# Streaming V in 8 MB tiles, wq in one load, and a tail with narrow last rows, in a one-core decode kernel

## The chip, the cores and the metric

The kernel runs on one core of one Trainium2 chip. The metric is the device time of one execution in microseconds (us). Before the change it was 405.86 us, the median of three runs (405.73 to 405.91). A profiled execution also has a span, from its first to its last instruction, which is some 1.8 us shorter than the time (404.1 against 405.84 us). "Clock" below is the granted clock of TensorE (PE), 1.0 for full and 0.5 for half. The other engines are DVE (VectorE), ACT (ScalarE) and POOL (GpSimd); PEld is the weight load of PE.

## The reference, cut to what matters

One token passes through an attention block (32 query heads, 4 KV heads, 65,536 cached keys of 128 values) and, beside it, a two-layer MLP. Both are added to the input.

```python
xn = layernorm(x)                                   # x: [1, 1, 1024] bf16
q = xn @ wq                                         # wq: [1024, 4096], 8.4 MB
p = softmax(q k^T * 128**-0.5)                      # k_cache: 67 MB
attn = (p @ v) @ wo                                 # v_cache: 67 MB, wo 8.4 MB
h = gelu(layernorm(xn) @ w1) ; x1 = xn + shift(h) @ w2   # shift: zero for one token
mlp = x1 + gelu(layernorm(x1) @ w3) @ w4            # w3, w4: 7.3 MB each
out = x + attn + mlp
```

Every byte of K, V and the weights is read once: 169.87 MB by the profile's count of its load queue. There is very little arithmetic per byte.

## The kernel before

All loads are issued on one queue in a fixed stream. K, V, wq, w3 and w4 share five tiles of 4 MB (32 KB per partition). The smaller matrices use one 2 MB tile. A load is issued as soon as its buffer is free.

```python
UKEYS = 16384
BIG_BUFS = 5
W4_PIECES = ((8, 8), (8, 2, 1, 1))
...
stream = [("wq", 0), ("wq", 1), ("w3", 0), ("w3", 1), ("w1", 0), ("K", 0), ("K", 1), ("V", 0)]
for u in range(2, NU):
    stream += [("K", u), ("V", u - 1)]
...
stream += [("wo", HKV - 1), ("V", NU - 1), ("w4", 0), ("w4", 1)]
...
src = cache[0, g, b * UKEYS:(b + 1) * UKEYS, :].rearrange("(p ct) d -> p (ct d)", p=P)
nc.sync.dma_start(out=t[:], in_=src)
```

The output is accumulated in psB, one tile of PSUM (the memory into which the matmuls write), whose rows 0 and 32 hold the two halves of the 1024 outputs. Each row of w2, wo and w4 adds two matmuls of 512 columns. w4 comes last, in pieces of 8, 8, 8, 2, 1 and 1 rows of 256 KB each, so that little work is left after the last byte.

```python
def row_acc(j, lhsT, rhs):
    nc.tensor.matmul(psB[32 * j:32 * j + 1, :], lhsT=lhsT, rhs=rhs, start=False, stop=False,
                     tile_position=(0, 32 * j), skip_group_check=True)
...
compute_w4(0, W4_PIECES[0][0])
compute_w4(1)
out_t = ppool.tile([64, 512], BF16, name="out_t", tag="p_sb")
nc.scalar.copy(out=out_t[:], in_=psB[0:64, :])
nc.scalar.dma_start(out=out[0, 0, :].rearrange("(j n) -> j n", j=2), in_=...)
```

## Time and profile before

| what | before |
|---|---|
| time, median | 405.86 us |
| span of the profiled execution | 404.1 us |
| data packets per DMA engine | 384 |
| load queue, first packet to last byte | 1.74 to 399.68: 397.94 us |
| of which packets fill, mean of 16 engines | 396.34 us |
| last byte to end of span | 4.37 us |

The last four rows are counted from the trace's records of single DMA packets. The window is the time from the first packet to the last byte. The packets leave 1.6 us of it empty, so faster compute could shorten it by no more than that. It is set by bytes and by the cost per packet.

Lines of the page of the kernel before: busy time of each engine, then, in 40 equal slices, the granted clock of PE in tenths and the busy share of the DMA engines in tenths, then the load queue.

```profile
span 404.1 us, 3287 instructions
PE 236.2 (58%) x1392; PEld 94.1 (23%) x1392; DVE 211.8 (52%) x241; ACT 34.3 (8%) x61; POOL 6.4 (2%) x19
...
PEclk9998558688897979797978979596959895879769
DMA  8999999999999999999999999999999999999993
...
q1 hardware_dynamic: 6912, 169.87, 98.1%
```

The DMA row is at 9 from the second slice to the second to last. No compute engine is busy for more than 58%.

The chain of waits of the kernel before (start, length, what), with its first piece, one of the long ones, and its end:

```profile
0.74 12.40 DMA x_bf<-in_A_x_dram
...
140.77 46.33 DMA big<-in_A_k_cache_dram
...
355.04 42.55 DMA big<-in_B_w_dram
397.63 2.93 PE psB L179 x24
400.58 0.58 ACT out_t L526
```

The chain ends in the last weight load and then in 24 matmuls. The timeline of the same stretch (start, length, engine, line, operation, output and inputs, count, and the idle time before):

```profile
394.19 1.89 PE L179 MATMUL psB<-big,cols_h 128*1 128x512 bf16 x16
...
397.63 2.91 PE L179 MATMUL psB<-big,cols_h 128*1 128x512 bf16 x24 [1.55 <-DMA big<-in_B_w_dram]
...
400.58 0.58 ACT L526 CAST out_t<-psB 64x512 bf16<-64x512 f32 x1 [25.40 <-PE psB L179]
401.19 0.61 ACTq L527 DMA_DIRECT2D out_dram<-out_t  x1
```

The last 24 matmuls took 2.9 us, about 0.12 us each, and kept pace with the last pieces. The busy time by stretch shows the clock they had (the column after POOL is the granted clock):

```profile
core 0: us, PE busy (x) PEld busy (x) DVE busy (x) ACT busy (x) POOL busy (x), PEclk, DMA share, GB/s
396.00:398.00 2.00, 0.45 (x6) 0.17 (x5) 0.00 (x0) 0.00 (x0) 0.00 (x0) 1.00 0.71 266
398.00:400.00 2.00, 2.00 (x22) 0.79 (x17) 0.00 (x0) 0.00 (x0) 0.00 (x0) 1.00 0.18 68
```

It was full.

### The profile page before, as it was taken

What the parts mean: (1) busy time and instruction counts of PE and PEld (TensorE: products, weight loads), DVE (VectorE), ACT (ScalarE), POOL (GpSimd) and SP (SyncE); (2) the same over time, 40 slices, a digit from 0 to 9 for tenths busy, and PEclk for the clock granted to TensorE, in tenths of its full rate; (3) what the DMA queues carried; (4) which work ended last, traced back from release to release, by engine and by line L of the source; (5) the groups of instructions that cost most, each with busy time, mean ns of one, the idle gap of its engine ahead of it and who ended that gap; (6) DMA issues with size and microseconds to landing.
All of it is one profiled execution on the core that took longest, in us unless ns stands there. A gap on an engine that the chain in (4) does not pass through costs nothing.

```text
span 404.1 us, 3287 instructions
## 1 busy us (share of the span) xinstructions
PE 236.2 (58%) x1392; PEld 94.1 (23%) x1392; DVE 211.8 (52%) x241; ACT 34.3 (8%) x61; POOL 6.4 (2%) x19
## 2 busy tenths in 40 slices
PE   0382727839483859292929394565658561948094
PEld 0131202313131323031313231122213220313041
DVE  0310046957658584566585473738393934665310
ACT  1000210110101011001010101010101010010100
POOL 4000100000000000000000000000000000000000
PEclk9998558688897979797978979596959895879769
DMA  8999999999999999999999999999999999999993
GB/s 357 422 415 431 449 416 439 440 418 429 448 417 425 454 409 430 444 431 417 448 428 418 436 420 438 428 444 423 428 436 428 422 436 435 431 426 430 420 427 144
DMA packets 7237, 170.11 MB, mean 421 GB/s; under 512 B 1070, under 2 KB 1074, under 8 KB 1462
## 3 DMA queue, kind: packets, MB, share of 16 engines
q1 hardware_dynamic: 6912, 169.87, 98.1%
q8 instruction: 11, 0.18, 0.2%
q0 software_dynamic: 160, 0.02, 0.0%
q10 hardware_dynamic: 150, 0.01, 0.0%
q14 instruction: 4, 0.03, 0.0%
HBM read 169.88 MB, written 0.01 MB: 420 GB/s over the span
## 4 chain that ended last, share of the span: by engine, by line
DMA 49%; PE 30%; DVE 10%; another core or an unknown queue 6%; ACT 2%; issue 2%; SPq 0%; DVEq 0%; ACTq 0%
DMA big<-in_A_k_cache_dram 35%; PE sc L383 21%; DMA big<-in_B_w_dram 11%; DVE big L372 5%; PE oacc L457 4%; DMA x_bf<-in_A_x_dram 3%; DVE s_sb L390 2%; PE psq L250 1%; ACT p_sb L421 1%; PE psB L179 1%; PE psB L239 1%; DVE pT L424 1%; PE pm_mx L400 1%; DVE og L439 0%
## 5 line engine op out<-in xcount | busy, mean ns | idle before, releaser
L383 PE MATMUL sc<-big,qdiag 128*128 128x512 bf16 x512 | 150.0, 461 | 104.9 <-DVE big L372 104.9
L372 DVE STREAM_TRANSPOSE big<-big 128x2048 f32<-128x2048 f32 x64 | 142.4, 2279 | 49.4 <-DMA big<-in_A_k_cache_dram 49.4
L383 PEld LDWEIGHTS <-qdiag 128*128 128x128 bf16 x512 | 56.8, 111 | 193.2 <-issue 100.3
L457 PE MATMUL oacc<-big,pT 128*32 128x512 bf16 x512 | 37.7, 396 | 9.7 <-DMA big<-in_A_v_cache_dram 9.7
L390 DVE TENSOR_SCALAR_CACHE_REDUCE s_sb<-sc 128x1024 f32<-128x1024 f32 x16 | 19.6, 1225 | 45.0 <-PE sc L383 45.0
L424 DVE STREAM_TRANSPOSE pT<-p_sb 128x1024 bf16<-128x1024 bf16 x16 | 19.8, 1240 | 16.8 <-ACT p_sb L421 16.8
L463 ACT COPY ob<-oacc 128x512 f32<-128x512 f32 x12 | 7.0, 586 | 214.6 <-PE oacc L457 214.6
L421 ACT ACTIVATE p_sb<-s_sb,nball 128x1024 bf16<-128x1024 f32 x16 | 18.4, 1150 | 76.5 <-DVE nball L419 76.5
L457 PEld LDWEIGHTS <-pT 128*32 128x32 bf16 x512 | 14.0, 99 | 28.7 <-issue 17.1
L400 PE MATMUL pm_mx<-ident_f,mx 128*1 128x128 f32 x16 | 4.3, 270 | 16.7 <-DVE s_sb L390 16.7
L419 DVE COPY nball<-pm_mx 128x1 f32<-128x1 f32 x16 | 2.5, 153 | 17.5 <-PE pm_mx L413 17.5
L250 PE MATMUL psh<-big,ln_rep_b 128*32 128x512 bf16 x56 | 5.5, 505 | 8.8 <-DMA big<-in_B_w_dram 8.8
L466 DVE SCALAR_TENSOR_TENSOR og<-oacc,wb,og 128x512 f32<-128x512 f32 x4 | 3.0, 751 | 12.5 <-PE oacc L457 12.5
L179 PE MATMUL psB<-big,cols_h 128*1 128x512 bf16 x56 | 7.7, 420 | 1.6 <-DMA big<-in_B_w_dram 1.6
L189 PE MATMUL pm_ln<-ln_rowsum_a,ones_f 128*128 128x1 f32 x2 | 0.6, 348 | 13.7 <-DVE sel L213 13.7
L179 PE MATMUL psB<-w,oT 128*1 128x512 bf16 x64 | 7.6, 379 | 0.0
L473 PE MATMUL pm_e<-og,selbig 128*128 128x128 f32 x32 | 5.6, 326 | 3.2 <-DVE nball L419 2.3
L402 DVE TENSOR_REDUCE negm<-pm_mx 1x8 f32<-1x128 f32 x16 | 4.4, 275 | 5.4 <-PE pm_mx L400 5.4
L250 PEld LDWEIGHTS <-ln_rep_b 128*32 128x32 bf16 x72 | 3.4, 120 | 15.0 <-issue 12.2
L183 DVE CAST xT<-x_bf 128x8 f32<-128x8 bf16 x1 | 0.2, 172 | 12.0 <-DMA x_bf<-in_A_x_dram 12.0
L400 PEld LDWEIGHTS pm_mx<-ident_f,mx 128*1 128x1 f32 x16 | 1.3, 79 | 21.9 <-DVE s_sb L390 21.9
L439 DVE SCALAR_TENSOR_TENSOR og<-ob,wb,og 128x512 f32<-128x512 f32 x8 | 6.0, 751 | 0.1
(98 smaller groups left out, 80.5 us busy)
## 6 DMA issues: line engine op xcount, KB each, us to landing
big<-in_A_k_cache_dram SPq DMA_DIRECT2D x16, 4096.0 KB, 46.1
big<-in_A_v_cache_dram SPq DMA_DIRECT2D x16, 4096.0 KB, 39.9
big<-in_A_wq_dram SPq DMA_DIRECT2D x2, 4096.0 KB, 16.9
w<-in_A_wo_dram SPq DMA_DIRECT2D x4, 2048.0 KB, 30.1
big<-in_B_w_dram SPq DMA_DIRECT2D x2, 3584.0 KB, 34.3
big<-in_B_w_dram SPq DMA_DIRECT2D x3, 2048.0 KB, 40.7
w<-in_B_w_dram SPq DMA_DIRECT2D x2, 2048.0 KB, 42.6
big<-in_B_w_dram SPq DMA_DIRECT2D x1, 512.0 KB, 43.4
```

The costliest lines, as they stand in the source:

```text
L179: nc.tensor.matmul(psB[32 * j:32 * j + 1, :], lhsT=lhsT, rhs=rhs, start=False, stop=False, tile_position=(0, 32 * j), skip_group_check=True)
L250: nc.tensor.matmul(acc[i][32 * q:32 * q + 32], lhsT=rep[:, c, :], rhs=wt[:, k, 512 * s:512 * (s + 1)], start=first, stop=last, tile_positi ...
L372: nc.vector.transpose(out=words, in_=words)
L383: nc.tensor.matmul(sc[:, sub, :], lhsT=qdiag[:, c0:c0 + P], rhs=cols[:, sub, s, :, b, :, r], start=(s == 0 and b == 0 and r == 0), stop=(s ...
L390: nc.vector.tensor_scalar(out=s_sb[:], in0=sc[:], scalar1=SCALE, scalar2=None, op0=ALU.mult, op1=ALU.max, accum_out=mx[:])
L400: nc.tensor.transpose(pm[0:1, 0:P], unit.pop((u, "mx"))[:, 0:1], ident_f[:])
L421: nc.scalar.activation(out=p_sb[:], in_=unit.pop((u, "ssb"))[:], func=ACTF.Exp, bias=nball[:, b:b + 1], scale=1.0, accum_out=group[(g, "la ...
L424: nc.vector.transpose(out=pT[:].rearrange("p u n -> p (u n)"), in_=p_sb[:].rearrange("p u n -> p (u n)"))
L439: nc.vector.scalar_tensor_tensor(out=og[:], in0=ob[:], scalar=wb[:, k:k + 1], in1=og[:], op0=ALU.mult, op1=ALU.add)
L457: nc.tensor.matmul(oacc[32 * q:32 * (q + 1), :], lhsT=pT[:, sub, 32 * t:32 * (t + 1)], rhs=vt[:, sub, :, t, :], start=(sub == 0 and t < 4) ...
L463: nc.scalar.copy(out=ob[:], in_=oacc[:])
L473: nc.tensor.matmul(pe[:, 0:P], lhsT=selbig[:, cg, :], rhs=og[:, 128 * cg:128 * (cg + 1)], start=(cg == 0), stop=(cg == 3))
```

## The change

Intended were fewer and larger descriptors for the 67 MB of V and for wq, with K in tiles of its own, and a shorter piece of work after the last byte. V is streamed in 8 MB tiles (64 KB per partition) through one buffer, K in 4 MB tiles through three. wq is one load. wo and w4 end in smaller pieces. Near the end psB is copied and spread by f32 matmuls over four column groups of 256, and the last four rows are added there by 256-wide matmuls. A column group is a tile position, `(0, 32 * j)`. The last V tile still comes in two halves of 32 KB rows.

```diff
-BIG_BUFS = 5
-W4_PIECES = ((8, 8), (8, 2, 1, 1))
+K_BUFS = 3
+W4_PIECES = ((4, 4, 4, 4), (4, 4, 2, 1, 1))
+LAST = 4
...
+    stream = [("wq", 0), ("w3", 0), ("w3", 1), ("w1", 0)]
+    for j in range(NU // 2):
+        stream += [("K", 2 * j), ("K", 2 * j + 1)]
...
+        stream.append(("V", j))
...
+                src = cache[0, g, b * UKEYS:(b + 2) * UKEYS, :].rearrange("(p ct) d -> p (ct d)", p=P)
+                if kind == "K":
+                    src = src[:, UKEYS * (i % 2):UKEYS * (i % 2 + 1)]
+                n = UKEYS if it == ("V", NU // 2 - 1) else src.shape[1]
+                for at in range(0, src.shape[1], n):
+                    nc.sync.dma_start(out=t[:, at:at + n], in_=src[:, at:at + n])
...
+    def close_out():
+        acc = opool.tile([64, 512], F32, name="acc", tag="ob")
+        nc.vector.tensor_copy(out=acc[:], in_=psB[0:64, :])
+        psC = ps_O.tile([P, 512], F32, name="psC", tag="oacc")
+        for j in range(4):
+            nc.tensor.matmul(psC[32 * j:32 * j + 32, 0:256], lhsT=ident_f[0:64, 32 * (j // 2):32 * (j // 2) + 32],
+                             rhs=acc[:, 256 * (j % 2):256 * (j % 2 + 1)], start=True, stop=False,
+                             tile_position=(0, 32 * j), skip_group_check=True)
+        ... the last LAST rows of w4, four matmuls of 256 columns each, into psC ...
...
-    compute_w4(1)
+    compute_w4(1, 0, sum(W4_PIECES[1]) - LAST)
+    psC = close_out()
```

More of the change, by code (lines that the diff above doesn't have):

```diff
@@ L60 @@
     small = ctx.enter_context(tc.tile_pool(name="small", bufs=2))
-    big = ctx.enter_context(tc.tile_pool(name="big", bufs=BIG_BUFS))
+    kpool = ctx.enter_context(tc.tile_pool(name="kt", bufs=K_BUFS))
+    vpool = ctx.enter_context(tc.tile_pool(name="vt", bufs=1))
     wts = ctx.enter_context(tc.tile_pool(name="wts", bufs=1))
@@ L64 @@
     ppool = ctx.enter_context(tc.tile_pool(name="psb", bufs=1))
-    ptpool = ctx.enter_context(tc.tile_pool(name="ptp", bufs=1))
+    ptpool = ctx.enter_context(tc.tile_pool(name="ptp", bufs=2))
     opool = ctx.enter_context(tc.tile_pool(name="ob", bufs=max(1, NB - 1)))
@@ L80 @@
     wo_v = A_wo.rearrange("(g p j) n -> g p j n", g=HKV, p=P)
-    stream = [("wq", 0), ("wq", 1), ("w3", 0), ("w3", 1), ("w1", 0), ("K", 0), ("K", 1), ("V", 0)]
-    for u in range(2, NU):
-        stream += [("K", u), ("V", u - 1)]
-        if u == 8:
+    stream = [("wq", 0), ("w3", 0), ("w3", 1), ("w1", 0)]
+    for j in range(NU // 2):
+        stream += [("K", 2 * j), ("K", 2 * j + 1)]
+        if j == NU // 2 - 1:
+            stream.append(("wo", HKV - 1))
+        stream.append(("V", j))
+        if j == 0:
             stream.append(("w2", 0))
-        if u % NB == 1:
-            stream.append(("wo", u // NB - 1)) if u > NB else None
-    stream += [("wo", HKV - 1), ("V", NU - 1), ("w4", 0), ("w4", 1)]
+        if j % 2 == 1 and j < NU // 2 - 1:
+            stream.append(("wo", j // 2))
+    stream += [("w4", 0), ("w4", 1)]
     class Stream:
@@ L93, in __init__ @@
             self.next = 0
-            self.held = {"big": 0, "wts": 0}
-            self.room = {"big": BIG_BUFS, "wts": 1}
+            self.held = {"k": 0, "v": 0, "wts": 0}
+            self.room = {"k": K_BUFS, "v": 1, "wts": 1}
             self.tiles = {}
         def pool_of(self, it):
-            return "wts" if it[0] in ("w1", "w2", "wo") else "big"
+            return {"K": "k", "w3": "k", "w4": "k", "V": "v", "wq": "v"}.get(it[0], "wts")
         def pump(self):
@@ L120, in load @@
                 src = {"w1": w1_v, "w2": w2_v}.get(kind)
-                nc.sync.dma_start(out=t[:], in_=wo_v[i] if src is None else src)
+                src = wo_v[i] if src is None else src
+                for lo, hi in ((0, 4), (4, 6), (6, 8)) if it == ("wo", HKV - 1) else ((0, 8),):
+                    nc.sync.dma_start(out=t[:, lo:hi], in_=src[:, lo:hi])
                 self.tiles[it] = t
                 return
-            t = big.tile([P, UKEYS], BF16, name="big")
+            if kind in ("V", "wq"):
+                t = vpool.tile([P, 2 * UKEYS], BF16, name="vt")
+            else:
+                t = kpool.tile([P, UKEYS], BF16, name="kt")
             self.tiles[it] = t
             if kind in ("K", "V"):
-                cache = A_k_cache if kind == "K" else A_v_cache
-                g, b = divmod(i, NB)
-                src = cache[0, g, b * UKEYS:(b + 1) * UKEYS, :].rearrange("(p ct) d -> p (ct d)", p=P)
-                nc.sync.dma_start(out=t[:], in_=src)
+                cache, j = (A_k_cache, i // 2) if kind == "K" else (A_v_cache, i)
+                g, b = divmod(2 * j, NB)
+                src = cache[0, g, b * UKEYS:(b + 2) * UKEYS, :].rearrange("(p ct) d -> p (ct d)", p=P)
[4 more added lines that the diff above has]
+                    nc.sync.dma_start(out=t[:, at:at + n], in_=src[:, at:at + n])
             elif kind == "wq":
-                nc.sync.dma_start(out=t[:], in_=wq_v[:, 4 * i:4 * i + 4, :].rearrange("p c n -> p (c n)"))
+                nc.sync.dma_start(out=t[:], in_=wq_v.rearrange("p c n -> p (c n)"))
             elif kind == "w3":
@@ L252, in row_matmul, with by_row, chunk, compute_wq @@
                                  tile_position=(0, 32 * q), skip_group_check=True)
-    def halves(t, width):
-        return t[:, 0:4 * width].rearrange("p (c n) -> p c n", c=4)
-    def chunk(i):
-        return [(4 * i + k, 4 * i + k == 0, 4 * i + k == DC - 1) for k in range(4)]
-    def compute_wq(i):
-        if i == 0:
-            vals["psq"] = ps_S.tile([P, SUBS, 512], F32, name="psq", tag="sc")
-        psq = [vals["psq"][:, e, :] for e in range(2)]
-        row_matmul(psq, xn_rep, halves(st.tiles[("wq", i)], HQ * DH), chunk(i), 8, lambda s: (s // 2, s % 2))
-        st.done(("wq", i))
-        if i == 0:
-            return
-        del vals["psq"]
+    def by_row(t, width, n):
+        return t[:, 0:n * width].rearrange("p (c n) -> p c n", c=n)
+    def chunk(i, n):
+        return [(n * i + k, n * i + k == 0, n * i + k == DC - 1) for k in range(n)]
+    def compute_wq():
+        psq = ps_S.tile([P, SUBS, 512], F32, name="psq", tag="sc")
+        psq = [psq[:, e, :] for e in range(2)]
+        row_matmul(psq, xn_rep, by_row(st.tiles[("wq", 0)], HQ * DH, DC), chunk(0, DC), 8, lambda s: (s // 2, s % 2))
+        st.done(("wq", 0))
         q_row = tmp.tile([P, 2, 512], BF16, name="q_row", tag="t")
@@ L301, in compute_w3 @@
         psh = [vals["psh"][:, e, :] for e in range(2)]
-        row_matmul(psh, xn2_rep, halves(st.tiles[("w3", i)], F), chunk(i), 7, lambda s: (s // 2, s % 2))
+        row_matmul(psh, xn2_rep, by_row(st.tiles[("w3", i)], F, 4), chunk(i, 4), 7, lambda s: (s // 2, s % 2))
         st.done(("w3", i))
@@ L319, in compute_w1 @@
         nc.scalar.activation(out=h1[:], in_=ps1[0:64], func=ACTF.Gelu_apprx_tanh)
-        g_rows = ptpool.tile([64, 512], BF16, name="g_rows", tag="pT")
+        g_rows = opool.tile([64, 512], BF16, name="g_rows", tag="ob")
         nc.vector.memset(g_rows[:], 0.0)
@@ L335, in compute_w2, with compute_w4 @@
         st.done(("w2", 0))
-    def compute_w4(i, lo=0, hi=None):
+    def compute_w4(i, lo, hi):
         wt = st.tiles[("w4", i)]
-        c0, n = sum(map(sum, W4_PIECES[:i])), sum(W4_PIECES[i])
-        hi = n if hi is None else hi
+        c0 = sum(map(sum, W4_PIECES[:i]))
         for k in range(lo, hi):
@@ L343, in compute_w4 @@
                 row_acc(j, vals["hT"][:, c0 + k:c0 + k + 1], wt[:, 1024 * k + 512 * j:1024 * k + 512 * (j + 1)])
-        if hi == n:
-            st.done(("w4", i))
+    def close_out():
[6 more added lines that the diff above has]
+                             tile_position=(0, 32 * j), skip_group_check=True)
+        wt = st.tiles[("w4", 1)]
+        for k in range(sum(W4_PIECES[1]) - LAST, sum(W4_PIECES[1])):
+            for j in range(4):
+                c = sum(W4_PIECES[0]) + k
+                nc.tensor.matmul(psC[32 * j:32 * j + 1, 0:256], lhsT=vals["hT"][:, c:c + 1],
+                                 rhs=wt[:, 1024 * k + 256 * j:1024 * k + 256 * (j + 1)], start=False, stop=(c == FC - 1),
+                                 tile_position=(0, 32 * j), skip_group_check=True)
+        return psC
     clock = [0]
@@ L450, in compute_v @@
             og, wb, lp = group_weights(g)
-        vt = st.tiles[("V", u)][:].rearrange("p (u s t d) -> p u s t d", u=SUBS, s=SETS, t=16)
-        oacc = ps_O.tile([P, 512], F32, name="oacc")
+        vt = st.tiles[("V", u // 2)][:].rearrange("p (e u s t d) -> e p u s t d", e=2, u=SUBS, s=SETS, t=16)[u % 2]
+        oacc = ps_O.tile([P, 512], F32, name="oacc", tag="oacc")
         pT = unit.pop((u, "pT"))
@@ L459, in compute_v @@
                                  stop=(sub == SUBS - 1 and t >= 12), tile_position=(0, 32 * q))
-        st.done(("V", u))
+        if u % 2 == 1:
+            st.done(("V", u // 2))
         if b < NB - 1:
@@ L504 @@
         if kind == "wq":
-            compute_wq(i)
+            compute_wq()
         elif kind == "w3":
@@ L514 @@
         elif kind == "V":
-            if i == NU - 1:
-                flush()
-            compute_v(i)
+            flush()
+            compute_v(2 * i)
+            compute_v(2 * i + 1)
+    half = sum(W4_PIECES[0]) // 2
     while waiting:
@@ L520 @@
         if waiting:
-            compute_w4(0, 0, W4_PIECES[0][0])
-    compute_w4(0, W4_PIECES[0][0])
-    compute_w4(1)
-    out_t = ppool.tile([64, 512], BF16, name="out_t", tag="p_sb")
-    nc.scalar.copy(out=out_t[:], in_=psB[0:64, :])
-    nc.scalar.dma_start(out=out[0, 0, :].rearrange("(j n) -> j n", j=2),
+            compute_w4(0, 0, half)
+    compute_w4(0, half, 2 * half)
+    compute_w4(1, 0, sum(W4_PIECES[1]) - LAST)
+    psC = close_out()
+    out_t = ppool.tile([P, 256], BF16, name="out_t", tag="p_sb")
+    nc.scalar.copy(out=out_t[:], in_=psC[:, 0:256])
+    nc.scalar.dma_start(out=out[0, 0, :].rearrange("(j n) -> j n", j=4),
                         in_=out_t[:].rearrange("(a b) n -> a b n", b=32)[:, 0, :])
```

## The prediction

> **What bounds the kernel.** The DMA engines. The page shows them at 90% or more in 38 of 40 slices; 169.87 MB on the load queue took 98.1% of 16 engines' span. In the trace's DMA records the load queue runs from 1.8 to 399.7 us of the 404.1 us span: 397.9 us, of which packets fill 396.3, so there is no starvation to remove. PE (58%) and DVE (52%) have slack; the chain of waits ends repeatedly in 42 to 49 us of "DMA <- K cache". The Trainium skill (DMA: Bandwidth & Descriptors, "Where 436 GB/s comes from") gives a ceiling of 435.2 GB/s: 390.3 us for 169.87 MB. The trace's 32 KB packet takes 1.215 us, on 16 engines 431.5 GB/s, so little is left. After the last weight byte come 0.4 us of psB matmuls, a 0.58 us ACT copy and the output DMA: 4.4 us in all.
>
> **The change, costed.**
> 1. V and wq rows go from 32 to 64 KB. Median packets are 0.613 us at 16 KB and 1.215 at 32 KB: 36.7 ns per 1000 bytes plus about 11 ns fixed. A 64 KB packet should take 2.42 us. Seven of eight V tiles (56 packets per engine) and wq (8) save 64 x 11 ns = 0.7 us. Smaller wo and w4 pieces add five loads, 40 packets per engine, 0.44 us. Net -0.3 us. K now reads 32 KB pieces at a 64 KB pitch; the old wq load has that pitch and its packets took 1.213 us: no cost.
> 2. One 8 MB V buffer, three K buffers. A V pair is consumed in about 4 us (1.85 us per 32 matmuls) after landing, while two K tiles (19.4 us of transfer) are queued or queueable: some 15 us of margin before the queue dries. K needs 9.3 us of matmuls plus 2.3 us of first transpose per tile. The softmax chain of the second K tile (about 5 us) ends near V's landing, so PE may run a few us late per pair without DMA cost.
> 3. Start: x_bf (8 tiny descriptors per engine on ACT's queue) alternates with the big packets: its records step by 1.21 us and it lands at 13.2 us. The skill's DMA page ("Queues, rings and completion order") says an engine round-robins between queues per packet; that agrees. With 64 KB packets each step is 2.42 us: x_bf should land at 22 to 24 us, and the first wq matmuls move from 22.7 to about 32. The freed buffers are needed only near 50 us: off the critical path.
> 4. Tail: psB is copied (0.7 us on DVE) and re-spread by f32 matmuls to four column groups while the last 1 MB (2.4 us) arrives; the last row is then four 256-wide matmuls (0.1 to 0.2 us instead of 0.4) and a 256-wide ACT copy (about 0.35 instead of 0.58). Gain 0.4 us if the f32 matmuls overlap; loss of about 0.5 if they run serially.
>
> **Predicted:** 405.86 - 0.3 - 0.3 = about 405.2 us, range 404.0 to 406.4. Chances: faster by over 2% 0.02, within 2% 0.96, slower 0.02.
>
> **Right or wrong in the profile:** V packets of 65,536 bytes at 2.42 us; DMA at 9 in all inner slices; load-queue window 397 to 398 us; x_bf landing past 20 us without a DMA gap; last byte to end 4.0 us rather than 4.4.
>
> **What would make it wrong:** 64 KB descriptors cut up or running at another rate (1% on V alone is 1.6 us); V freed later than 15 us after landing, seen as lower DMA slices at each pair; serial f32 matmuls.

## The result, and the profile after

The changed kernel took 406.67 us in the median of four runs (405.59, 406.28, 407.06, 407.07), and the kernel before 405.81 us (405.73 to 405.91, four runs). The ratio is 1.0017, 95% interval 0.9995 to 1.0039. A ratio here is the mean time of one kernel's runs over that of the other's of the same rounds, so it is not quite the ratio of the medians quoted. The 390.3 us in the prediction is an estimate from the ceiling that the Trainium skill states there; the measured window of 397.94 us for 169.87 MB is 426.9 GB/s. The interval of the ratio includes 1, so the change is not shown to be slower. The class (within 2%) was right. The time missed the range of 404.0 to 406.4 us by 0.3 us, on the side opposite to the predicted gain. The runs of the changed kernel also spread over 1.5 us, where those of the kernel before spread over 0.2 us.

| what | before | after | predicted for after |
|---|---|---|---|
| span of the profiled execution | 404.05 | 405.27 | |
| data packets per DMA engine | 384 | 360 | 360 (64 saved, 40 added) |
| median packet of 64 KB | none | 2.420 us | 2.42 us |
| load queue window | 397.94 | 398.10 | 397 to 398 |
| packets fill | 396.34 | 396.23 | |
| last byte to end of span | 4.37 | 5.44 | 4.0 |

The page of the changed kernel, the same lines as before:

```profile
span 405.3 us, 3307 instructions
PE 250.4 (62%) x1408; PEld 95.5 (24%) x1408; DVE 210.6 (52%) x242; ACT 35.3 (9%) x61; POOL 6.4 (2%) x19
...
PEclk9999868767768868886988687669877876787786
DMA  9989999989999999999999999999999999999992
...
q1 hardware_dynamic: 6480, 169.87, 97.8%
```

The prediction had 9 in all inner slices of the DMA row; the third and the ninth are at 8, but this is no drain of the queue. The window is only 0.16 us longer than before, and packets leave 1.9 us of it empty instead of 1.6. The chain of waits of the changed kernel:

```profile
0.74 22.16 DMA x_bf<-in_A_x_dram
...
84.89 6.32 PE oacc L482 x50
91.20 0.02 issue
91.22 37.62 DMA vt<-in_A_v_cache_dram
...
399.39 0.69 DVE acc L357
400.08 0.14 issue
400.22 1.08 PE psC L360 x8
401.30 0.98 PE psC L367 x16
```

x_bf lands at 22.9 us as predicted. V is given back 6.3 us after its work starts rather than 4 us, because its matmuls ran at half clock, but that is still far inside the margin. The timeline of the tail:

```profile
395.01 1.03 PE L193 MATMUL psB<-kt,cols_h 128*1 128x512 bf16 x8 [1.47 <-DMA kt<-in_B_w_dram]
...
397.48 1.87 PE L193 MATMUL psB<-kt,cols_h 128*1 128x512 bf16 x8 [1.44 <-DMA kt<-in_B_w_dram]
...
399.39 0.68 DVE L357 COPY acc<-psB 64x512 f32<-64x512 f32 x1 [10.06 <-PE psB L193]
...
400.22 1.08 PE L360 MATMUL psC<-acc,ident_f 64*32 64x256 f32 x8 [0.87 <-DVE acc L357]
...
402.30 0.37 ACT L554 CAST out_t<-psC 128x256 bf16<-128x256 f32 x1 [21.51 <-PE psC L367]
```

Eight matmuls that took 1.03 us at 395.0 take 1.87 us at 397.5. The copy, the re-spread and the 16 narrow matmuls can only follow. The last byte landed at 399.83 us, and the last matmul ended 2.4 us later, where it had been 0.9 us before (400.55 less 399.68). The stretches name the reason:

```profile
396.00:398.00 2.00, 0.56 (x6) 0.22 (x5) 0.00 (x0) 0.00 (x0) 0.00 (x0) 0.88 0.67 252
398.00:400.00 2.00, 1.35 (x8) 0.13 (x2) 0.61 (x1) 0.00 (x0) 0.00 (x0) 0.50 0.16 62
```

The clock went to half at 397.5 us by the clock record, as the last 4-row piece landed. The re-spread was to run while the last 1 MB arrives, but it began at 400.22 us, after the last byte.

### The profile page after: what moved, and what is told of

Same layout as the page of the kernel before. It is cut to its first block, busy times and chain, and to the rows that moved or that the text cites. A ratio compares the mean times of both kernels' runs of the same rounds, so it can differ in the third digit from the quotient of the medians. Undisturbed runs are those within 1.5% of the kernel's fastest.

```text
span 405.3 us, 3307 instructions
## 1 busy us (share of the span) xinstructions
PE 250.4 (62%) x1408; PEld 95.5 (24%) x1408; DVE 210.6 (52%) x242; ACT 35.3 (9%) x61; POOL 6.4 (2%) x19
## 3 DMA queue, kind: packets, MB, share of 16 engines
q1 hardware_dynamic: 6480, 169.87, 97.8%
## 4 chain that ended last, share of the span: by engine, by line
DMA 82%; PE 14%; DVE 2%; SPq 1%; issue 0%; ACT 0%
DMA vt<-in_A_v_cache_dram 46%; DMA kt<-in_A_k_cache_dram 11%; DMA w<-in_A_wo_dram 10%; DMA kt<-in_B_w_dram 8%; PE oacc L482 8%; DMA x_bf<-in_A_x_dram 5%; PE sc L408 2%; PE psq L264 1%; PE psB L253 1%; DVE kt L397 1%; PE psB L193 0%; PE psh L264 0%; SPq L128 0%; PE pm_ln L203 0%; PE pm_ln L212 0%
## 5 line engine op out<-in xcount | busy, mean ns | idle before, releaser
L408 PE MATMUL sc<-kt,qdiag 128*128 128x512 bf16 x512 | 152.3, 461 | 71.0 <-DVE kt L397 70.7
L397 DVE STREAM_TRANSPOSE kt<-kt 128x2048 f32<-128x2048 f32 x64 | 144.3, 2286 | 67.9 <-DMA kt<-in_A_k_cache_dram 67.9
L408 PEld LDWEIGHTS <-qdiag 128*128 128x128 bf16 x512 | 55.9, 111 | 158.3 <-issue 87.9
L482 PE MATMUL oacc<-vt,pT 128*32 128x512 bf16 x512 | 48.2, 557 | 14.1 <-DMA vt<-in_A_v_cache_dram 14.1
L482 PEld LDWEIGHTS <-pT 128*32 128x32 bf16 x512 | 17.8, 132 | 40.7 <-issue 23.7
L197 DVE CAST xT<-x_bf 128x8 f32<-128x8 bf16 x1 | 0.2, 170 | 22.9 <-DMA x_bf<-in_A_x_dram 22.9
L193 PE MATMUL psB<-kt,cols_h 128*1 128x512 bf16 x48 | 8.1, 454 | 3.3 <-DMA kt<-in_B_w_dram 3.3
L438 PE MATMUL pm_mx<-ident_f,rep 1*128 1x1 f32 x16 | 3.8, 235 | 5.0 <-DVE rep L430 5.0
```

Of the source, the lines that this page charges most:

```text
L397: nc.vector.transpose(out=words, in_=words)
L408: nc.tensor.matmul(sc[:, sub, :], lhsT=qdiag[:, c0:c0 + P], rhs=cols[:, sub, s, :, b, :, r], start=(s == 0 and b == 0 and r == 0), stop=(s ...
L482: nc.tensor.matmul(oacc[32 * q:32 * (q + 1), :], lhsT=pT[:, sub, 32 * t:32 * (t + 1)], rhs=vt[:, sub, :, t, :], start=(sub == 0 and t < 4) ...
```

## The experiments

My theory: the stream is neutral to slightly better, and the time is set by the clock that the tail happens to find. The rival: the 64 KB rows or the single V buffer cost the time and make it vary. All kernels gave correct results. Each timed batch ran on one chip together with runs of the kernel before.

### The stream without the new tail

```diff
-W4_PIECES = ((4, 4, 4, 4), (4, 4, 2, 1, 1))
+W4_PIECES = ((8, 8), (8, 2, 1, 1))
...
-    psC = close_out()
...             # wo and w4 in the old pieces, psB copied out 64x512 as before
```

> The changed kernel with its tail undone: wo and w4 in the old pieces, psB copied out 64x512 as before; the 8 MB V tiles, the 64 KB rows and the single wq load stay. Theory (the streaming half is neutral, the new tail at half TensorE clock costs the time): about 405.4 to 405.9 us with a spread like the kernel before (within 0.3 us), load-queue window 397.6 to 398.2 us, last byte to end 4.4 us. Rival (the 64 KB rows or the single V buffer cost the time and make it vary): 406.5 us or more, and run-to-run spread above 1 us stays.

Measured: 405.64 us in the median of six (405.58, 405.59, 405.63, 405.66, 406.66, 408.06), ratio 0.9993 (0.9964 to 1.0021). Window 397.68 us, last byte to end 4.43 us, 320 packets per engine. The median and the window are as the theory said. The spread was not: two of six runs were 1 and 2.4 us late (406.66 and 408.06 us). But the kernel before did the same in that batch, with 8 of 11 runs at 405.7 to 406.0 us and three at 407.3 to 408.3. So an occasional late end is not new with the change, and the four runs of the kernel before at the prediction had all been early ones. The profile is of an early run. Its timeline is needed further down:

```profile
392.48 1.89 PE L190 MATMUL psB<-kt,cols_h 128*1 128x512 bf16 x16 [0.56 <-DMA kt<-in_B_w_dram]
397.40 2.88 PE L190 MATMUL psB<-kt,cols_h 128*1 128x512 bf16 x24 [3.04 <-DMA kt<-in_B_w_dram]
```

### The new tail without the stream

```diff
-W4_PIECES = ((8, 8), (8, 2, 1, 1))
+W4_PIECES = ((4, 4, 4, 4), (4, 4, 2, 1, 1))
+LAST = 4
...
+    psC = close_out()      # BIG_BUFS = 5 and the 4 MB K and V tiles stay
```

> The kernel before with the new tail alone (small wo and w4 pieces, last four rows in four column groups after the f32 re-spread); K and V stay in 4 MB tiles with five shared buffers. Theory (tail at half clock): 406.3 to 407.3 us, or near 405.6 in runs in which the tail finds the clock full, so a spread of about 1 us; last byte to end 5.4 us when the clock record shows 0.5 after the last byte. Rival (streaming costs it): 405.4 to 405.9, spread within 0.3.

Measured: 407.17 us (406.48, 406.68, 406.81, 407.52, 407.53, 407.74), ratio 1.0016 (0.9991 to 1.0041). Not one of six runs was as early as the usual run of the kernel before. The expected early runs near 405.6 us did not come, and three runs lay above the expected 407.3 us. The new tail without the stream thus carries a loss, but it has two parts. It adds 40 packets per engine to the old 384, and the window is 398.64 us instead of 397.94. Of the 0.84 us by which the profiled run is longer, 0.70 us are window and only 0.15 us the end after the last byte. No profile fell on one of the three runs above 407.5 us. In the profile, which is one of the earlier runs, the clock fell at 399.7 us, the re-spread took 1.08 us and the narrow matmuls 1.02 us. The expected figure of 5.4 us from last byte to end was for a clock of 0.5 throughout. Here only the second half of the tail had it, and it was 4.5 us.

### The changed kernel with TensorE kept busy

```diff
+    def keep_warm(i, n):        # results go to a scratch PSUM tile that nobody reads
+        for k in range(n):
+            nc.tensor.matmul(dump[32 * (k % 2):32 * (k % 2) + 1, 0, :], lhsT=vals["hT"][:, 0:1],
+                             rhs=st.tiles[("w4", i)][:, 0:512], start=True, stop=True, ...)
...
+    keep_warm(0, 8)             # after the first w4 tile
+    keep_warm(1, 8)             # after rows 0-3 of the second
+    keep_warm(1, 4)             # after rows 4-7
```

> The changed kernel with 20 matmuls whose result nobody reads, put into the gaps in which TensorE waits for the last w4 pieces, to hold its clock. Theory: the clock stays at 1.0 until the end, the f32 re-spread is done before the last piece lands, last byte to end 4.0 us, time about 405.3 us with spread within 0.3. Rival (serial chain too long even at full clock, or the streaming part): 406.3 or more with last byte to end above 5 us although the clock is 1.0.

Measured: 405.51 us, all six runs within 405.39 to 405.63. The ratio is 0.9976 (0.9951 to 1.0002). Last byte to end 4.13 us. From the timeline of this kernel:

```profile
395.93 1.46 PE L548 MATMUL dump<-kt,cols_h 128*1 128x512 bf16 x12
397.56 1.03 PE L193 MATMUL psB<-kt,cols_h 128*1 128x512 bf16 x8 [0.17 <-DMA kt<-in_B_w_dram]
399.46 0.64 PE L360 MATMUL psC<-acc,ident_f 64*32 64x256 f32 x8 [0.87 <-DVE acc L357]
400.02 0.61 PE L367 MATMUL psC<-kt,cols_h 128*1 128x256 bf16 x16
```

Added work took the spread away. It did not lower the median: in the same batch the plain change, run again in the next section, had 405.47 us, with two of six runs late. The eight matmuls are back to 1.03 us, the re-spread from 1.08 to 0.64 us and the narrow ones from 1.02 to 0.61 us. The scheduler moved eight of the 20 fillers to before 393 us, but the other twelve filled the gap before 397.5 us. The clock record stays at 1.0 to the end of the work. Even so the re-spread ended at 400.10 us, after the last byte at 399.53 us, and the gain over the 4.37 us of the kernel before was 0.24 us.

### The changed kernel again

No edit.

> The changed kernel unaltered, for a second profile and its spread. Theory: times between 405.5 and 407.1 us; if this profile ends near 405.6 its clock in the last 5 us is 1.0 and last byte to end about 4.2 us, if near 407 the clock is 0.5 and it is about 5.4 us; the load-queue window is the same 398 us in both. Rival: the window moves by 1 us with the time and the end does not.

Measured: 405.36, 405.39, 405.44, 405.49, and 407.22, 407.34 us; median 405.47, ratio 0.9989 (0.9961 to 1.0017). The profile was of the run of 407.22 us: clock 0.50 from 397.3 us on, last byte to end 5.65 us, window 398.04 us. In this batch the same kernel thus has two ways to end, about 1.8 us apart, and its median depends on which of them the few runs of a batch show. In this one it is 0.46 us below that of the kernel before, in the first result it was 0.86 us above.

### The kernel before with fillers: first attempt

```diff
+    keep_warm(12)               # into a scratch tile, from tiles long resident, between the two w4 tiles
```

> The kernel before with 12 matmuls that nobody reads between the two w4 tiles, over the gap in which TensorE waits for the last 8-row piece. Theory (the slow executions of the kernel before, 407.3 to 408.3 us, are ones in which its last 24 matmuls ran at half clock): all runs at 405.7 to 406.1 us, none above 407. Rival (the slow executions come from the transfers or from elsewhere): about one run in four still above 407.

Measured: 405.86, 405.91, 406.06, 406.10, 407.20 and 408.38 us; the ratio was 1.0015 (0.9995 to 1.0036). It failed as a test. The answer on the filler's tile shows where the fillers went:

```profile
L522 PE MATMUL dump<-qdiag,cols_h x12: 377/378/379, 370.2 to 373.8; 128*1 128x512 bf16 x12
```

Nothing tied them to the tail, and they ran at 370 to 374 us, 20 us too early.

### The kernel before with fillers held in place

```diff
+    def keep_warm(n):
+        for k in range(n):
+            row_acc(k % 2, qdiag[:, 0:1], qdiag[:, 0:512])   # zero weights into psB: result unchanged
...
     compute_w4(0, W4_PIECES[0][0])
+    keep_warm(12)
     compute_w4(1)
```

> The kernel before with 12 matmuls of zero weights into psB (result unchanged), held in place by psB itself between the two w4 tiles, since the fillers of the earlier attempt were scheduled 20 us too early. Theory (slow executions of the kernel before are a half clock in its last 24 matmuls): all runs at 405.7 to 406.1 us. Rival: about one run in four still above 407 us, so the slow executions come from elsewhere or the filler does not hold the clock.

Measured: 405.80 to 405.98 us in all five runs, median 405.96, ratio 0.9996 (0.9983 to 1.001). In the same batch one of nine runs of the plain kernel took 407.03 us. From its timeline:

```profile
395.81 1.46 PE L179 MATMUL psB<-qdiag 128*1 128x512 bf16 x12
397.80 2.88 PE L179 MATMUL psB<-big,cols_h 128*1 128x512 bf16 x24 [0.53 <-DMA big<-in_B_w_dram]
```

With the gap at 0.53 us instead of 1.55 us the late ends did not occur, and the clock was 1.0 from 391.5 us to the end. But at a rate of about one late run in six (below), five early runs come up by chance in 40% of cases. So this run alone does not show that the fillers prevent them. The next look shows what a late end is.

### One more look at the kernel before

No edit.

> The kernel before unaltered, for one more profile. Theory: either 405.7 to 406.0 us with the last 24 matmuls in 2.9 us at clock 1.0, or (one in four) 407.2 to 408.3 us with clock 0.5 and the last 24 matmuls in about 5 us. Rival: a slow one with clock 1.0 in the tail.

Measured: 407.22 us (one run, state unknown), one of its late executions. Its window is 398.12 us, its last byte to end 5.58 us instead of 4.37. From its timeline, and the busy time of one stretch:

```profile
392.90 1.89 PE L179 MATMUL psB<-big,cols_h 128*1 128x512 bf16 x16 [0.41 <-DMA big<-in_B_w_dram]
397.83 4.10 PE L179 MATMUL psB<-big,cols_h 128*1 128x512 bf16 x24 [3.04 <-DMA big<-in_B_w_dram]
```

```profile
398.00:400.00 2.00, 2.00 (x12) 0.61 (x10) 0.00 (x0) 0.00 (x0) 0.00 (x0) 0.50 0.19 71
```

The last 24 matmuls took 4.1 us, for 2.9 in the first profile. The clock was half from 397.2 to 400.6 us, and came back for the rest. This is the same kernel with the same stream. PE had been at full clock from 386.9 us, finished its earlier rows sooner, and then sat idle for 3.04 us. In the first profile the clock had risen only at 391.8 us, PE was late with its backlog and idle for only 1.55 us, and the clock held. But the idle time alone does not decide: the version with the old tail had the same 16 matmuls, the same 3.04 us of waiting and the same 24 matmuls, only some 0.4 us earlier, and they took 2.88 us at a clock of 1.0. The section on the clock record says what differed.

### One more look at the changed kernel

No edit.

> The changed kernel unaltered, for one more profile. Theory: either 405.4 to 405.6 us with clock 1.0 in the last 6 us and last byte to end near 4.1 us, or 407.0 to 407.4 us with clock 0.5 and last byte to end 5.4 to 5.7 us; the load-queue window 398.0 us in either. Rival: 407 us with clock 1.0 or 405.4 us with clock 0.5.

Measured: 406.58 us (one run, state unknown), between the two values that I had expected. The clock fell at 399.2 us, so the eight matmuls at 397.75 us still took 1.03 us, while the re-spread took 1.08 and the narrow ones 1.02 us. Last byte to end 4.94 us, window 398.03 us. So there is a range of ends, set by when the clock falls, and not two values only. My expectation of two values was wrong; that the clock decides the end was not.

### Four column groups from the beginning, long and short rows

Here psB is kept in four column groups of 256 throughout, so that nothing needs to be re-spread. The w4 pieces are the large ones of the kernel before.

```diff
-    def row_acc(j, lhsT, rhs):
-        nc.tensor.matmul(psB[32 * j:32 * j + 1, :], lhsT=lhsT, rhs=rhs, start=False, stop=False, ...)
+    def row_acc(lhsT, row):
+        for j in range(4):
+            nc.tensor.matmul(psB[32 * j:32 * j + 1, 0:256], lhsT=lhsT, rhs=row[:, 256 * j:256 * (j + 1)],
+                             start=False, stop=False, tile_position=(0, 32 * j), skip_group_check=True)
```

On the changed stream (8 MB V tiles, 64 KB rows):

> The 8 MB V tiles and 64 KB rows with the large w4 pieces of the kernel before, and psB kept as four column groups of 256 from the beginning, so that there is no f32 re-spread. Theory: window 397.7 us, last byte to end 4.0 to 4.1 us whatever the clock, so 405.1 to 405.4 us in all runs. Rival (slow runs do not come from matmuls after the last pieces): spread above 1 us stays.

On the kernel before (4 MB tiles in five shared buffers, 32 KB rows):

> The kernel before (4 MB tiles, five shared buffers, 32 KB rows) with psB in four column groups of 256 from the beginning. Theory: last byte to end 4.0 to 4.1 us, window 397.9 to 398.0, so 405.4 to 405.7 us in all runs, 0.2 to 0.5 us above the one with long rows. Rival (V tiles of 8 MB cost something): equal to or faster than the one with long rows.

On the changed stream, with every V tile and wq loaded as two halves of 32 KB rows:

> As the narrow one with long rows, but every V tile and wq loaded in two halves of 32 KB rows: same buffers, same order, only the descriptor size differs. Theory: 64 more packets per engine at about 11 ns give 0.5 to 0.7 us of packet time; the time is 0.2 to 0.7 us longer. x_bf lands at 13 us instead of 23 and the first wq matmuls start near 23 us instead of 33, without any gain from that. Rival (the late x_bf costs time): this one is the faster of the two.

| kernel | times, five runs | ratio to before | packets per engine | window | packets fill | last byte to end |
|---|---|---|---|---|---|---|
| narrow, 64 KB rows | 405.29 to 405.76 | 0.9984 (0.9973 to 0.9996) | 320 | 397.53 | 395.70 | 4.26 |
| narrow, before's tiles | 405.65 to 405.94 | 0.9993 (0.9981 to 1.0005) | 384 | 397.99 | 396.36 | 4.24 |
| narrow, 8 MB tiles in 32 KB rows | 406.21 to 406.73 | 1.0009 (0.9997 to 1.0021) | 384 | 398.16 | 396.54 | 4.63 |

The spread of all three is at most 0.52 us. The expectations were a little too good: the time from last byte to end of the first two was 4.26 and 4.24 us and not 4.0 to 4.1, and one run of the first and four of the second lay above their ranges. In all three profiles the clock was half when the last weights were added, so these tails are quick enough at half clock. From the timeline and a stretch of the first of them:

```profile
397.27 2.87 PE L191 MATMUL psB<-kt,cols_h 128*1 128x256 bf16 x48 [3.89 <-DMA kt<-in_B_w_dram]
```

```profile
398.00:400.00 2.00, 2.00 (x40) 1.05 (x29) 0.00 (x0) 0.00 (x0) 0.00 (x0) 0.50 0.15 52
```

With four column groups at half clock the last 12 rows kept the pace that two groups had at full clock (2.87 us here, 2.91 us in the first profile of the kernel before). The first and the third differ in descriptor size alone. 64 packets fewer per engine save 0.84 us of packet time and 0.63 us of window. The first against the second saves 0.66 and 0.46 us. The second's median is 0.42 us above the first's, as expected. The third's is 1.0 us above it, more than the 0.7 us expected. In the profile some 0.4 us of that is the time from the output's packet to the end, which I cannot explain.

The same pair answers the question of the late x_bf. The first use of x_bf in the long-row kernel, then in the short-row kernel:

```profile
22.86 0.17 DVE L195 CAST xT<-x_bf 128x8 f32<-128x8 bf16 x1 [22.86 <-DMA x_bf<-in_A_x_dram]
```

```profile
13.18 0.17 DVE L196 CAST xT<-x_bf 128x8 f32<-128x8 bf16 x1 [13.18 <-DMA x_bf<-in_A_x_dram]
```

The kernel in which x_bf lands 9.7 us later is the faster one, so the late landing costs nothing that shows.

### The re-spread moved forward

```diff
-LAST = 4
+LAST = 12
```

> The changed kernel with the f32 re-spread moved before the whole second w4 tile (12 narrow rows instead of 4), so that the serial chain of psB copy and re-spread runs while 3 MB more are arriving. Theory: last byte to end 4.0 to 4.3 us whatever the clock, all runs at 405.3 to 405.7 us, no run above 406.5. Rival (the narrow last rows or the small pieces themselves cost it): runs near 407 remain.

Measured: 405.38 to 405.52 us in all five runs, median 405.44, ratio 0.9984 (0.9972 to 0.9997). Last byte to end 3.88 us. From its timeline:

```profile
394.60 0.64 PE L360 MATMUL psC<-acc,ident_f 64*32 64x256 f32 x8 [0.87 <-DVE acc L357]
```

The same copy and re-spread now run at 393.8 to 395.2 us, while 3 MB are still on their way. The clock fell at 399.5 us in this profile and only the last eight matmuls felt it. One number changed, and the variation is gone. The small pieces and the narrow rows are therefore not the fault in themselves. The number does two things at once, though: it moves the re-spread forward, and it makes eight more rows narrow, which shortens the work on them. No run separates the two. What the late ends of the changed kernel contain is the serial chain of eight matmuls, copy, re-spread and 16 matmuls that has to fit into the last 1 MB, or 2.4 us. At full clock it nearly does: 1.03 + 0.68 + 0.64 is 2.35 us, and then come the 0.61 us of narrow matmuls, the last of which must wait for the last byte anyway. At half clock it is 1.87 + 0.68 + 1.08 + 1.02, or 4.7 us.

### What the clock record says

The clock record changes in steps of 3.413 us. I cut all 14 full-length profiles into these windows and took, for each, the share of it in which a matmul was in flight, and the clock of the window after it. Of 914 windows at full clock, 626 were followed by full clock, with shares from 0.42 up (0.48 at the 5th percentile). The 288 that were followed by half clock had shares up to 0.57 (0.43 at the 95th percentile). Of 602 at half clock, the 279 that were followed by full clock had shares of 0.76 or more, and the other 323 of 0.76 or less. Between 0.42 and 0.57 both happened. Ends of matmuls are modelled in these traces, so I take the shares to be good to a few hundredths, as an estimate.

That sorts the tails. In the first profile of the kernel before, the window from 395.2 us had a share of 0.54 and the clock stayed. In its late execution the window from 393.8 us had 0.30, and the clock fell at 397.2 us. In the version with the old tail, with the same work at nearly the same times, the windows began at 392.8 and 396.2 us, the first had 0.46, and the clock stayed. By this count the same work and the same gap end differently because the windows cut them differently. In the changed kernel a 4-row piece arrives about every 2.5 us and keeps PE busy for 1.03 us, about 42%. That is right at the edge. In its first profile the window from 394.1 us had 0.31 and the clock fell at 397.5 us. In the look at 406.58 us one window had 0.45 and kept the clock, and the next, also 0.45, lost it. The Trainium skill ("TensorE: Matmul & The Clock Gate", "Part 1: The HAM clock gate") says the window is free-running and does not restart with the kernel. The records agree: the boundaries fall at other places in each profile (397.5, 397.3 and 399.2 us for the fall in the three of the changed kernel). So the end can vary from run to run.

Over all batches, six of 36 runs of the kernel before were above 406.5 us, and five of 11 of the changed kernel. These counts are too small to show that the change made late ends more frequent (by Fisher's exact test, one-sided, chance alone gives such a difference in some 6% of cases), and in the batch that had most of them they were 2 of 6 against 3 of 11. But the three versions of the changed stream that fill the gap, move the re-spread forward or need none (with the long rows) had no run above 405.8 us in 16, against five late ones in 11 of the changed kernel. The early ends of the changed kernel (405.36 to 405.59) are below those of the kernel before (405.65 to 406.14), by about 0.4 us; one run of the changed kernel, 406.28 us, lies between early and late.

## Why the prediction was right or wrong

- **DMA bound, no starvation to remove.** Right. The windows of all profiles go with the packets per engine, whatever the buffers: 397.53 and 397.68 us at 320, 397.78 to 398.10 at 360, 397.94 to 398.16 at 384, 398.64 at 424.
- **Step 1, descriptors.** Right in mechanism and about right in size. A 64 KB packet takes 2.420 us (2.42 predicted), and the counts are 384 to 360. The 64 saved packets gave 0.84 and 0.66 us of packet time in the two comparisons (0.7 predicted). The 40 added ones are the difference between the changed kernel and its version with the old tail: 396.23 less 395.80, 0.43 us (0.44 predicted); added to the kernel before they took more, 397.00 less 396.34, 0.66 us. The net of -0.3 us did not show in the window, which was 397.94 and 398.12 us before and 398.10, 398.04 and 398.03 us after. A net this small lies at the scatter of the window.
- **Step 2, buffers.** Right in its result: the queue never dried. The 4 us for a V pair were 6.3 us in the first one, since I used the full-clock 1.85 us per 32 matmuls. The margin covered it.
- **Step 3, x_bf.** Right: 22.9 us (22 to 24 predicted), first wq matmuls at 32.8 us (about 32), no cost.
- **Step 4, tail.** This is the step that failed. I put it at "Gain 0.4 us if the f32 matmuls overlap; loss of about 0.5 if they run serially", and entered -0.3 us, for 4.0 us from last byte to end. The three profiles of the changed kernel have 5.44, 5.65 and 4.94 us. The f32 matmuls did run side by side: the eight of them, in four column groups, took 0.64 us at full clock. What failed is that copy and re-spread would run while the last 1 MB arrives. The copy has to wait for the eight matmuls of the last 4-row piece, which the prediction left out, and the re-spread ended 1.0 to 1.7 us after the last byte. The second error is in leaving the clock out: I had assumed the full clock of the one profile I had. The chain is 3.0 us at full and 4.7 us at half clock, and the change's own 4-row pieces put PE on the edge of losing it. With the clock held at full by the fillers the end took 4.13 us, 0.24 us less than before, so even there the gain was smaller than the 0.4 us. No profile fell on an early execution of the changed kernel; that those at 405.4 us kept the full clock is likely from the fillers' 405.51 us, but not shown.
- **The range.** I took the 0.2 us spread of three runs as that of the kernel. It has late executions in one run of six, by 1.1 to 2.4 us, and the changed kernel had five in 11. That the first four runs of the changed kernel came out 0.86 us slower is luck in part: in the second batch its median was 0.46 us below that of the kernel before, near the 0.6 us predicted.

Not shown is why two of six runs of the version with the old tail were late; no profile fell on one of them. Its tail is that of the kernel before, so the same cause is likely, but that is argued and not measured. Nor did a profile fall on an execution above 407.3 us. The latest ones, near 408.3 us, are 2.4 us late, where the profiled one is 1.4 us late; by an estimate from the 1.87 us that eight such matmuls took at half clock, 24 would take 5.6 us instead of 2.9, which would be enough.

## What to carry to other kernels

In a kernel that waits for transfers to the end, cost the work after the last byte at both clocks of TensorE. Whether a profile shows full or half clock there can be luck of that one execution. Then move serial steps (copies, re-spreads) to before the wait, or use column groups so that even half clock keeps pace. Both took the variation away here, and with the long rows both gave 0.9984 of the time before. Filler matmuls held the clock too where a data dependency kept them in place; without one they ran 20 us too early.

## What the Trainium skill lacked or had wrong

- "TensorE: Matmul & The Clock Gate", sections "Part 1: The HAM clock gate" and "HAM oscillation", says the clock is halved after at least one idle window of about 3.4 us, with the abstract rule "no PE-idle gaps >~3.4µs". The window length agrees (3.413 us steps in the clock record). As a rule on single gaps it is too mild: in the changed kernel the clock fell with no gap longer than 1.5 us, and in the version with the old tail it held over a gap of 3.04 us. What the records show is a share: every full-clock window with less than about 0.42 of its time busy lost the clock, none above 0.57 did, and from half clock about 0.76 was needed to regain it (1,516 windows of 14 profiles). The page does say, in "A second HAM failure mode: psum-queue depth-cycling", that frequent short idle times make the clock swing, but it gives no share.
- The same page (Part 1) says that for modelling the warm-up ramp costs under 1% of a typical span. It speaks of a kernel's start and not of its end. The late ends here are under 1% as well (1.1 to 2.4 us of 406), but that is more than the gain that the change was to bring, and which of them a batch caught decided the sign of its median.
- "DMA: Bandwidth & Descriptors", "Queues, rings and completion order", gives round-robin between queues at packet granularity, with 9 to 17 descriptors as a typical packet. The trace agrees on the round-robin, but here a turn was one descriptor: the 16-byte records of x_bf come one by one, 1.21 us apart beside 32 KB packets and 2.42 us beside 64 KB ones. The consequence, which the section does not spell out, is that a small load with eight descriptors per engine waits for eight large packets, so it landed at 13.2 us beside 32 KB packets and at 22.9 us beside 64 KB ones.
- The same page, "Bandwidth", gives about 10.5 ns per packet, as a floor of tiny transfers issued from GpSimd. That passage says nothing of large packets. A similar figure came out for them here: medians of 0.613, 1.215 and 2.420 us at 16, 32 and 64 KB leave about 11 ns fixed per packet, and 64 packets fewer per engine saved 0.66 to 0.84 us.
